# Five operand sums of a Strassen-form MoE layer moved to the tensor engine, and a Sinkhorn normalisation re-placed: one Trainium2 core

## The chip, the cores and the metric

The kernel runs on one core of one Trainium2 chip. The metric is the device time of one execution in microseconds (us): the kernel before takes 2233.35 us, the median of three runs (2232.98 to 2233.5). The times and views below come from the hardware profiler's record of one further execution, which took 2235.71 us, of which the span from the first to the last instruction is 2233.9 us.

## The reference, cut to what matters

```python
# banded attention with ALiBi slopes, 4 batches x 8 heads x 768 positions x 64
x = attention(q, k, v).transpose(0, 2, 1, 3).reshape(3072, 512)
logits = x @ w_gate                        # 3072 x 8
P = np.exp(logits - logits.max())
for _ in range(8):                         # Sinkhorn
    P /= P.sum(1, keepdims=True) + 1e-09   # rows
    P /= P.sum(0, keepdims=True) + 1e-09   # columns
    P *= N / E                             # 3072 / 8
out = 0
for e in range(8):                         # every expert, dense
    h  = np.maximum(x @ w1[e], 0.0)        # 512 -> 1024
    out += P[:, e:e+1] * (h @ w2[e])       # 1024 -> 512
```

All of it is float32. The column sums run over all 3072 rows, so no expert with a scale can be added up before the last token has been through attention and all eight iterations have ended.

## The kernel before, in words

**Precision.** An operand of a matmul is kept as a high part (rounded to the matmul's float32r format) and a low part (what is left), and a product is three matmuls: high x low, low x high, high x high (`products`, L601).

**Stages.** The 3072 rows are handled as 8 units of 384 rows (3 tiles of 128). `pipeline` (L750) first runs the attention unit by unit. Between its steps it fills in two kinds of work: the first half of expert 0 for the units already done (`filler`, L823: four first-layer tiles `h_ps`, L616, then three second-layer tiles `y_ps`, L683), and the operand sums for the Strassen form (`combine`, L584, its GpSimd branch, L596 to L599). Then comes the main part: the rest of expert 0 and experts 1 to 7, in 30 groups of 256 hidden columns, for three blocks of 1024 rows. The last block is done first, because its rows are still in SBUF (`passes`, L932).

**A group.** `layer1_strassen` (L630) makes the first layer of one group with seven products m1 to m7 of 6 matmuls each, into four PSUM banks a, b, c, d. The products take sums and differences of row tiles ("tile pairs"): m1, m6 and m7 take sums (`SUMS`, L761), m4 and m3 differences, which are written over the tiles they are made from (`DIFFERENCES`, L762). `second` (L946) then makes the second layer, 8 tiles of 6 matmuls, one group behind the first layer. From group 2 on (expert 1) each of its tiles is scaled by a column of `pm`, the Sinkhorn result (L962), and expert 0's part is scaled once (L961).

**The handover.** The last two tile pairs of the last block come from the last units of attention. Their three sums and two differences are made after attention, by `last_pairs` (L905), which calls `combine` with `hurry`: GpSimd adds the low parts (`xres`, L589), VectorE the high parts (`xsum`, L591) and the two together (L592), ScalarE rounds to the new high part (L593), VectorE subtracts to get the new low part (L594). In program order: the sums (L909), ten loads of sums made earlier (L910), the last unit's gate (L913), and the last unit's expert-0 filler (L916), with the differences between its two layers (L832), because they overwrite rows that the filler's first layer still reads.

**Sinkhorn.** `sinkhorn` (L716) is a generator. Each `next` issues one part: the maximum of the logits (three parts), then per iteration the row part (L735 to L738 on VectorE) and, in the next part, a matmul with ones for the column sums (`c_ps`, L741) and the column part (L743 to L747 on VectorE). Its sums `rsum` and `csum` are SBUF tiles. It takes 11 calls: four in the last filler (L918), the others in `second`, before every other tile (L955), from group 0's second layer on.

**What sets the order.** Each engine works through its own queue in order. The queues are written at compile time by a planner that simulates the program and takes, on each engine, what it thinks ready, earlier program order first. From group 3's first layer on, the tensor engine's matmuls stay in program order (`InOrder`, L79); the handover, Sinkhorn and groups 0 to 2 are in the planner's hands. PSUM in this part: four banks with tag "h" (`mps`, for `h_ps` and the banks a to d), three with tag "y" (`yps`), one with tag "s" (`sps`, for the gate and Sinkhorn).

Of the kernel before, what the change touches and what calls it, by code (L numbers as in the profile page):

```python
# [8 lines left out]
F32 = mybir.dt.float32  # L9
F32R = mybir.dt.float32r  # L10
I32 = mybir.dt.int32
AF = mybir.ActivationFunctionType
ALU = mybir.AluOpType
# [4 lines left out]
P = 128  # L18
# [483 lines left out]
class Moe:  # L502
# [4 lines left out]
    def __init__(self, tc, const, ident, w_gate, w1, w2, out):  # L507
        self.tc, self.nc = tc, tc.nc
        nc = self.nc
        self.ident, self.w1, self.w2, self.out = ident, w1, w2, out  # L510
        self.E, self.DM, self.DF = w1.shape
        self.KT = self.DM // P
        self.KH = self.KT // 2
        self.N = out.shape[0]
        self.NU = self.N // UNIT
        E = self.E
        self.g_f = const.tile([P, self.KT, E], F32, name="g_f")
        self.ghl = const.tile([P, self.KT, P], F32R, name="ghl")
        self.w_gate = w_gate
        self.ones = const.tile([P, P], F32, name="ones")  # L520
        nc.gpsimd.memset(self.ones, 1.0)
        TT = self.N // P
        self.lg = const.tile([P, TT, E], F32, name="lg")
        self.pm = const.tile([P, TT, E], F32, name="pm")
        self.small = const
        self.pe = nc.tensor

    def load_gate(self):
        nc, E, ghl = self.nc, self.E, self.ghl
        nc.sync.dma_start(out=self.g_f, in_=self.w_gate.rearrange("(c p) e -> p c e", p=P))  # L530
        nc.gpsimd.memset(ghl.bitcast(F32), 0.0)
        nc.gpsimd.tensor_copy(out=ghl[:, :, 0:E], in_=self.g_f)
        nc.gpsimd.tensor_tensor(out=ghl[:, :, E:2 * E], in0=self.g_f, in1=ghl[:, :, 0:E], op=ALU.subtract)

    def stage_pair(self, e, f, stage):
# [47 lines left out]

    def combine(self, dst, x, y, op, tmp, hurry):  # L584

        nc, n = self.nc, dst[0].shape[1]
        s = tmp.tile([P, 2, self.KH, P], F32, name="xsum")[:, 0:n]
        r = tmp.tile([P, 2, self.KH, P], F32, name="xres")[:, 0:n]
        nc.gpsimd.tensor_tensor(out=r, in0=x[1], in1=y[1], op=op)  # L589
        if hurry:  # L590
            nc.vector.tensor_tensor(out=s, in0=x[0], in1=y[0], op=op)  # L591
            nc.vector.tensor_tensor(out=s, in0=s, in1=r, op=ALU.add)  # L592
            nc.scalar.copy(out=dst[0], in_=s)  # L593
            nc.vector.tensor_tensor(out=dst[1], in0=s, in1=dst[0], op=ALU.subtract)  # L594
        else:
            nc.gpsimd.tensor_tensor(out=s, in0=x[0], in1=y[0], op=op)  # L596
            nc.gpsimd.tensor_tensor(out=dst[0], in0=s, in1=r, op=ALU.add)
            nc.gpsimd.tensor_tensor(out=s, in0=s, in1=r, op=ALU.add)
            nc.gpsimd.tensor_tensor(out=dst[1], in0=s, in1=dst[0], op=ALU.subtract)  # L599

# [28 lines left out]

    def layer1_strassen(self, x, w, hs, tmp, ps, tag, sums_first):  # L630

# [21 lines left out]
        if not sums_first:  # L653
            product("m1", "a", True, False)
        tt(out=h22, in0=a, in1=t3, op=ALU.add)
        if not sums_first:
            product("m6", "b", True, True)
        tt(out=b, in0=b, in1=h22, op=ALU.add)
        product("m5", "c", False, True)
        product("m4", "d", False, True)  # L660
        tt(out=t3, in0=d, in1=t3, op=ALU.add)
# [54 lines left out]
    def sinkhorn(self, ps, tag):  # L716
# [14 lines left out]
        nc.vector.tensor_scalar(out=gm, in0=ngm_ps, scalar1=-1.0, scalar2=None, op0=ALU.mult)  # L731
        nc.scalar.activation(out=pm, in_=lg, func=AF.Exp, bias=gm, scale=1.0)
        for _ in range(SINKHORN_ITERS):
            rsum = small.tile([P, TT], F32, name="rsum")
            nc.vector.tensor_reduce(out=rsum, in_=pm, op=ALU.add, axis=AX.X)  # L735
            nc.vector.tensor_scalar(out=rsum, in0=rsum, scalar1=EPS, scalar2=None, op0=ALU.add)
            nc.vector.reciprocal(out=rsum, in_=rsum)
            nc.vector.tensor_tensor(out=pm, in0=pm, in1=rsum.unsqueeze(2).broadcast_to([P, TT, E]), op=ALU.mult)  # L738
            yield
            c_ps = ps.tile([P, TT, E], F32, name="c_ps", tag=tag)  # L740
            self.pe.matmul(c_ps, lhsT=ones, rhs=pm, start=True, stop=True)  # L741
            csum = small.tile([P, E], F32, name="csum")
            nc.vector.tensor_reduce(out=csum, in_=c_ps.rearrange("p t e -> p e t"), op=ALU.add, axis=AX.X)  # L743
            nc.vector.tensor_scalar(out=csum, in0=csum, scalar1=EPS, scalar2=None, op0=ALU.add)
            nc.vector.reciprocal(out=csum, in_=csum)
            nc.vector.tensor_scalar(out=csum, in0=csum, scalar1=float(N) / E, scalar2=None, op0=ALU.mult)
            nc.vector.tensor_tensor(out=pm, in0=pm, in1=csum.unsqueeze(1).broadcast_to([P, TT, E]), op=ALU.mult)  # L747


def pipeline(tc, attention, ident, moe, acc, scratch):  # L750
# [12 lines left out]
    with ExitStack() as top:  # L763
# [23 lines left out]
        def block(m, c, n):  # L787

            k, i = BLOCKS[m]
            return tuple(ring[s][k][:, c + i:c + 2 * n:2] for s in range(2))  # L790
# [10 lines left out]
        def combo(m, x, y, op, p, n):  # L801
            c, b, q = 2 * p % RT, p // WT, slice(p % WT, p % WT + n)
            new = tuple(xout.tile([P, 2, KH, P], F32R, name=name)[:, 0:n] for name in ("oh", "ol"))
            moe.combine(new, block(x, c, n), block(y, c, n), op, xtmp, False)
            spills.extend((op_spill[b][m][s][:, q], new[s]) for s in range(2))
# [17 lines left out]
        def filler(u, ps1, tag1, ps2, tag2, dst=None):  # L823
# [7 lines left out]
            if dst is not None:  # L831
                last_pairs(DIFFERENCES, ALU.subtract, lambda m: block(m, LAST, 2))  # L832
            for t in range(UT):
# [70 lines left out]

        def last_pairs(ms, op, dst):  # L905
            for m, x, y in ms:
                moe.combine(dst(m), block(x, LAST, 2), block(y, LAST, 2), op, xtmp, True)

        last_pairs(SUMS, ALU.add, lambda m: tuple(a[:, 2:4] for a in ops[0][m]))  # L909
        for m in ("m1", "m6", "m7", "m4", "m3"):  # L910
            for s in range(2):
                dma(ops[0][m][s][:, 0:2], op_spill[NB - 1][m][s][:, 0:2])
        for _ in moe.gate(NU - 1, xs[NU - 1], sps, "s", sps, "s"):  # L913
            pass
        sinkhorn = moe.sinkhorn(sps, "s")
        for n, _ in enumerate(filler(NU - 1, mps, "h", yps, "y", acc[:, BT - UT:])):  # L916
            if n % 6 == 5:
                next(sinkhorn, None)  # L918
        fill.close()
# [26 lines left out]
        def second(g, b, hs):  # L946
            e = groups[g % NG][0]
            first_scaled = e != 0 and groups[g % NG - 1][0] == 0
            for i in range(2):
                for t in range(WT):  # L950
                    j = 2 * t + i
                    tt = b * BT + j
                    y_ps = moe.layer2(t, wts[g], hs[i], yps, "y")
                    if t % 2 == 0:
                        next(sinkhorn, None)  # L955
                    a = acc[:, j]
# [12 lines left out]
        for n, (g, b) in enumerate(steps):  # L969
# [3 lines left out]
            if p > 0 and g % NG == 0:  # L973
# [3 lines left out]
                prev = None  # L977
            hs = moe.layer1_strassen(ops[p % 2], wts[g], h_sets[n % 2], tmp, mps, "h", n == 0)
            if g + 1 < len(steps) and g + 1 not in wts:
# [79 lines left out]
```

## Time and profile before

| what | value |
|---|---|
| median of 3 runs | 2233.35 us |
| profiled execution, whole / span | 2235.71 / 2233.9 us |
| tensor engine busy | 2194.8 us (98%) |
| VectorE / GpSimd / ScalarE busy | 1358.9 / 1126.3 / 769.0 us |
| granted tensor clock, mean | 0.99 |
| end of attention and background filler on the tensor engine | about 344 us |
| first product of group 0 (m1) | 363.25 us |
| first and last Sinkhorn matmul | 371.85 and 448.13 us |
| first row block scaled by `pm` | 451.75 us |

A row of the timeline reads: start in us, duration in us, engine, source line, operation, output <- inputs, shape, count, and in brackets the idle time just before it with what ended it. PE is the tensor engine's matmul, PEld its weight load, DVE is VectorE, ACT ScalarE, POOL GpSimd, SP the queue that issues DMAs. A matmul's duration overlaps the next one's; what counts for throughput is the distance from start to start. L86 is a helper through which all in-order matmuls go. A tile's rows give minimum/median/maximum duration in ns. Rows of the windows view give busy time of each engine in a stretch, the number of instructions, and the granted tensor clock. The times lie in one execution, the median over three others.

### The profile page before, as it was taken

What the parts mean: (1) busy time and instruction counts of PE and PEld (TensorE: products, weight loads), DVE (VectorE), ACT (ScalarE), POOL (GpSimd) and SP (SyncE); (2) the same over time, 40 slices, a digit from 0 to 9 for tenths busy, and PEclk for the clock granted to TensorE, in tenths of its full rate; (3) what the DMA queues carried; (4) which work ended last, traced back from release to release, by engine and by line L of the source; (5) the groups of instructions that cost most, each with busy time, mean ns of one, the idle gap of its engine ahead of it and who ended that gap; (6) DMA issues with size and microseconds to landing.
All of it is one profiled execution on the core that took longest, in us unless ns stands there. A gap on an engine that the chain in (4) does not pass through costs nothing.

```text
span 2233.9 us, 29587 instructions
## 1 busy us (share of the span) xinstructions
PE 2194.8 (98%) x10887; PEld 1817.9 (81%) x10887; DVE 1358.9 (61%) x2382; ACT 769.0 (34%) x1562; POOL 1126.3 (50%) x1050
## 2 busy tenths in 40 slices
PE   8999998999999999999999999999999999999999
PEld 5888886778888888888888888888888888888887
DVE  5555556866566656655666666566556665666665
ACT  6676763223222322223222222222232232222221
POOL 5575575545454545445544545454555455544540
PEclk8999999999999999999999999999999999999999
DMA  6566554111111111162111111111521111111111
GB/s 157 160 168 180 150 161 162 39 48 48 57 48 57 48 57 48 57 221 89 49 49 55 51 54 48 57 48 57 167 88 47 57 48 57 48 51 54 50 46 49
DMA packets 224842, 177.68 MB, mean 80 GB/s; under 512 B 119728, under 2 KB 187824, under 8 KB 224688
## 3 DMA queue, kind: packets, MB, share of 16 engines
q1 hardware_dynamic: 224688, 175.70, 25.6%
q8 instruction: 87, 1.43, 0.3%
q14 instruction: 67, 0.55, 0.1%
HBM read 146.56 MB, written 29.10 MB: 79 GB/s over the span
## 4 chain that ended last, share of the span: by engine, by line
PE 93%; ACT 3%; DVE 3%; issue 1%; DMA 0%; SPq 0%; DVEq 0%; ACTq 0%
PE y_ps L86 45%; PE bank_a L86 11%; PE bank_d L86 10%; PE bank_c L86 10%; PE bank_b L86 5%; PE h_ps L86 2%; PE o_ps L86 2%; PE t_ps L89 2%; PE s_ps L86 1%; ACT p_sb L300 1%; PE tp L89 1%; DVE kl L249 0%; PE r_ps L89 0%; PE g_ps L86 0%; ACT kh L248 0%
## 5 line engine op out<-in xcount | busy, mean ns | idle before, releaser
L962 DVE SCALAR_TENSOR_TENSOR acc<-y_ps,pm,acc 128x512 f32<-128x512 f32 x672 | 502.7, 748 | 244.5 <-PE y_ps L86 243.3
L545 POOL TENSOR_TENSOR wl<-wsum,wh 128x1280 fp32r<-128x1280 f32 x90 | 266.1, 2957 | 556.2 <-ACT wh L544 556.2
L567 POOL TENSOR_TENSOR wsum<-w1f 128x256 f32<-128x256 f32 x450 | 318.0, 741 | 318.6 <-DMA w1f<-in_moe_w_dram 318.5
L86 PE MATMUL y_ps<-w2h,h_set 128*128 128x512 f32 x1408 | 434.7, 390 | 0.0
L86 PE MATMUL y_ps<-w2h,x 128*128 128x512 f32 x1408 | 433.5, 389 | 0.0
L544 ACT CAST w2h<-w2f 128x1024 fp32r<-128x1024 f32 x90 | 94.8, 1054 | 687.8 <-issue 612.2
L86 PEld LDWEIGHTS y_ps<-w2h,h_set 128*128 128x128 f32 x1408 | 265.2, 188 | 55.2
L86 PEld LDWEIGHTS y_ps<-w2h,x 128*128 128x128 f32 x1408 | 264.3, 188 | 54.9
L86 PE MATMUL y_ps<-w2l,h_set 128*128 128x512 f32 x704 | 274.9, 390 | 3.9 <-DVE acc L962 3.9
L86 PE MATMUL y_ps<-w2l,x 128*128 128x512 f32 x704 | 273.9, 389 | 0.0
L86 PE MATMUL bank_a<-m,wh 128*128 128x512 f32 x696 | 242.8, 389 | 1.0 <-DVE h_set L613 1.0
L545 POOL TENSOR_TENSOR w2l<-w2f,w2h 128x1024 fp32r<-128x1024 f32 x90 | 216.5, 2406 | 53.0 <-ACT w2h L544 53.0
L86 PE MATMUL bank_d<-x,wh 128*128 128x512 f32 x696 | 242.6, 389 | 0.0
L86 PE MATMUL bank_c<-x,wh 128*128 128x512 f32 x696 | 242.5, 389 | 0.0
L652 DVE TENSOR_TENSOR scratch<-scratch,bank_d 128x512 f32<-128x512 f32 x90 | 61.9, 688 | 175.1 <-PE bank_d L86 171.4
L86 PEld LDWEIGHTS y_ps<-w2l,h_set 128*128 128x128 f32 x704 | 132.7, 188 | 31.7 <-DVE acc L962 4.2
L86 PEld LDWEIGHTS y_ps<-w2l,x 128*128 128x128 f32 x704 | 132.1, 188 | 27.4
L86 PEld LDWEIGHTS bank_a<-m,wh 128*128 128x128 f32 x696 | 130.6, 188 | 29.0 <-DVE h_set L613 1.9
L86 PEld LDWEIGHTS bank_c<-x,wh 128*128 128x128 f32 x696 | 130.6, 188 | 27.1
L86 PEld LDWEIGHTS bank_d<-x,wh 128*128 128x128 f32 x696 | 130.6, 188 | 27.0
L86 PE MATMUL bank_a<-m,wl 128*128 128x512 f32 x348 | 135.4, 389 | 0.0
L86 PE MATMUL bank_d<-x,wl 128*128 128x512 f32 x348 | 135.4, 389 | 0.0
(230 smaller groups left out, 3568.4 us busy)
## 6 DMA issues: line engine op xcount, KB each, us to landing
w1f<-in_moe_w_dram SPq DMA_DIRECT2D x92, 512.0 KB, 3.4
w2f<-in_moe_w_dram SPq DMA_DIRECT2D x92, 512.0 KB, 3.6
x<-op_m SPq DMA_DIRECT2D x16, 512.0 KB, 7.9
m<-op_m SPq DMA_DIRECT2D x12, 512.0 KB, 8.1
out_dram<-acc SPq DMA_DIRECT2D x24, 256.0 KB, 4.0
ys<-y_sb SPq DMA_DIRECT2D x21, 256.0 KB, 2.2
acc<-ys SPq DMA_DIRECT2D x21, 256.0 KB, 4.1
op_m<-oh SPq DMA_DIRECT2D x30, 128.0 KB, 1.9
```

Of the source, the lines that this page charges most:

```text
L86: return self.tc.keep_in_program_order(self.engine.matmul(*args, **kw))
L89: return self.tc.keep_in_program_order(self.engine.transpose(*args, **kw))
L300: nc.scalar.activation(out=pv, in_=pv, func=AF.Exp, bias=mx[:, u:u + 1], scale=-1.0, accum_out=sm[:, i, j:j + 1])
L544: self.nc.scalar.copy(out=hi, in_=full)
L545: self.nc.gpsimd.tensor_tensor(out=lo, in0=full, in1=hi, op=ALU.subtract)
L567: nc.gpsimd.tensor_tensor(out=s[:, n], in0=x, in1=y, op=op)
L652: tt(out=t3, in0=t3, in1=d, op=ALU.subtract)
L962: nc.vector.scalar_tensor_tensor(out=a, in0=y_ps, scalar=moe.pm[:, tt, e:e + 1], in1=a, op0=ALU.mult, op1=ALU.add)
```

## The change

1. `combine` loses its `hurry` branch. A new `combine_fast` makes the last two pairs' sums and differences by four matmuls into one PSUM bank of tag "h": identity x high part of x, plus or minus identity x high part of y, and the same for the low parts. ScalarE rounds the bank to the new high part, VectorE subtracts for the new low part. GpSimd has no share in it. A constant `plus_minus` (identity and its negative) is made by two GpSimd instructions when the gate weights are loaded.
2. `last_pairs(SUMS, ...)` is called after the ten loads and the last unit's gate instead of before them.
3. In Sinkhorn, `rsum` and `csum` are columns of the same PSUM bank as `c_ps`, which is now allocated at the row part. The factor N/E is folded into the tensor_scalar ahead of the reciprocal (L744), so L746 goes.
4. `layer1_strassen` gets a `beat` that issues one part of Sinkhorn, called twice in each first layer; `second` issues a part before its tiles t == 2 only (two per group instead of four). The four calls in the last filler stay.

```diff
+        self.plus_minus = const.tile([P, 2, P], F32R, name="plus_minus")
...
+        nc.gpsimd.tensor_copy(out=self.plus_minus[:, 0], in_=self.ident)
+        nc.gpsimd.tensor_scalar(out=self.plus_minus[:, 1], in0=self.ident, scalar1=-1.0, scalar2=None, op0=ALU.mult)
...
+    def combine_fast(self, dst, x, y, minus, ps, tag):
+
+        nc = self.nc
+        s = ps.tile([P, 2, self.KH, P], F32, name="x_ps", tag=tag)
+        one, other = self.plus_minus[:, 0], self.plus_minus[:, int(minus)]
+        for m, (w, a) in enumerate(((one, x[0]), (other, y[0]), (one, x[1]), (other, y[1]))):
+            self.pe.matmul(s, lhsT=w, rhs=a, start=(m == 0), stop=(m == 3))
+        nc.scalar.copy(out=dst[0], in_=s)
+        nc.vector.tensor_tensor(out=dst[1], in0=s, in1=dst[0], op=ALU.subtract)
...
         if not sums_first:
             product("m1", "a", True, False)
+        beat()
         tt(out=h22, in0=a, in1=t3, op=ALU.add)
...
         product("m5", "c", False, True)
+        beat()
         product("m4", "d", False, True)
...
+        cols = TT * E
         for _ in range(SINKHORN_ITERS):
-            rsum = small.tile([P, TT], F32, name="rsum")
+            bank = ps.tile([P, cols + TT + E], F32, name="c_ps", tag=tag)
+            c_ps, rsum, csum = bank[:, 0:cols], bank[:, cols:cols + TT], bank[:, cols + TT:]
...
-            nc.vector.tensor_scalar(out=csum, in0=csum, scalar1=EPS, scalar2=None, op0=ALU.add)
+            nc.vector.tensor_scalar(out=csum, in0=csum, scalar1=EPS, scalar2=float(E) / N, op0=ALU.add, op1=ALU.mult)
             nc.vector.reciprocal(out=csum, in_=csum)
-            nc.vector.tensor_scalar(out=csum, in0=csum, scalar1=float(N) / E, scalar2=None, op0=ALU.mult)
...
-        last_pairs(SUMS, ALU.add, lambda m: tuple(a[:, 2:4] for a in ops[0][m]))
         for m in ("m1", "m6", "m7", "m4", "m3"):
             for s in range(2):
                 dma(ops[0][m][s][:, 0:2], op_spill[NB - 1][m][s][:, 0:2])
         for _ in moe.gate(NU - 1, xs[NU - 1], sps, "s", sps, "s"):
             pass
+        last_pairs(SUMS, False, lambda m: tuple(a[:, 2:4] for a in ops[0][m]))
         sinkhorn = moe.sinkhorn(sps, "s")
+
+        def beat():
+            next(sinkhorn, None)
...
-                    if t % 2 == 0:
-                        next(sinkhorn, None)
+                    if t == 2:
+                        beat()
```

More of the change, by code (lines that the diff above doesn't have):

```diff
@@ L582, in strassen_pair, with combine @@
         return wh, wl, w2h, w2l
-    def combine(self, dst, x, y, op, tmp, hurry):
+    def combine(self, dst, x, y, op, tmp):
         nc, n = self.nc, dst[0].shape[1]
@@ L589, in combine @@
         nc.gpsimd.tensor_tensor(out=r, in0=x[1], in1=y[1], op=op)
[L590 to L599, printed above, removed]
+        nc.gpsimd.tensor_tensor(out=s, in0=x[0], in1=y[0], op=op)
+        nc.gpsimd.tensor_tensor(out=dst[0], in0=s, in1=r, op=ALU.add)
+        nc.gpsimd.tensor_tensor(out=s, in0=s, in1=r, op=ALU.add)
+        nc.gpsimd.tensor_tensor(out=dst[1], in0=s, in1=dst[0], op=ALU.subtract)
+    def combine_fast(self, dst, x, y, minus, ps, tag):
[6 more added lines that the diff above has]
+        nc.vector.tensor_tensor(out=dst[1], in0=s, in1=dst[0], op=ALU.subtract)
     def products(self, out, hi, lo, xhi, xlo, n, first, last):
@@ L628, in layer1, with layer1_strassen @@
             yield 3 * UNIT
-    def layer1_strassen(self, x, w, hs, tmp, ps, tag, sums_first):
+    def layer1_strassen(self, x, w, hs, tmp, ps, tag, sums_first, beat):
         nc, KH = self.nc, self.KH
@@ L739, in sinkhorn @@
             yield
-            c_ps = ps.tile([P, TT, E], F32, name="c_ps", tag=tag)
             self.pe.matmul(c_ps, lhsT=ones, rhs=pm, start=True, stop=True)
-            csum = small.tile([P, E], F32, name="csum")
-            nc.vector.tensor_reduce(out=csum, in_=c_ps.rearrange("p t e -> p e t"), op=ALU.add, axis=AX.X)
-            nc.vector.tensor_scalar(out=csum, in0=csum, scalar1=EPS, scalar2=None, op0=ALU.add)
+            nc.vector.tensor_reduce(out=csum, in_=c_ps.rearrange("p (t e) -> p e t", e=E), op=ALU.add, axis=AX.X)
+            nc.vector.tensor_scalar(out=csum, in0=csum, scalar1=EPS, scalar2=float(E) / N, op0=ALU.add, op1=ALU.mult)
             nc.vector.reciprocal(out=csum, in_=csum)
-            nc.vector.tensor_scalar(out=csum, in0=csum, scalar1=float(N) / E, scalar2=None, op0=ALU.mult)
             nc.vector.tensor_tensor(out=pm, in0=pm, in1=csum.unsqueeze(1).broadcast_to([P, TT, E]), op=ALU.mult)
@@ L803, in combo @@
             new = tuple(xout.tile([P, 2, KH, P], F32R, name=name)[:, 0:n] for name in ("oh", "ol"))
-            moe.combine(new, block(x, c, n), block(y, c, n), op, xtmp, False)
+            moe.combine(new, block(x, c, n), block(y, c, n), op, xtmp)
             spills.extend((op_spill[b][m][s][:, q], new[s]) for s in range(2))
@@ L831, in filler @@
             if dst is not None:
-                last_pairs(DIFFERENCES, ALU.subtract, lambda m: block(m, LAST, 2))
+                last_pairs(DIFFERENCES, True, lambda m: block(m, LAST, 2))
             for t in range(UT):
@@ L903, in pipeline, with last_pairs @@
         ops[0].update({m: block(m, FIRST, WT) for m in BLOCKS})
-        def last_pairs(ms, op, dst):
+        def last_pairs(ms, minus, dst):
             for m, x, y in ms:
-                moe.combine(dst(m), block(x, LAST, 2), block(y, LAST, 2), op, xtmp, True)
-        last_pairs(SUMS, ALU.add, lambda m: tuple(a[:, 2:4] for a in ops[0][m]))
+                moe.combine_fast(dst(m), block(x, LAST, 2), block(y, LAST, 2), minus, mps, "h")
         for m in ("m1", "m6", "m7", "m4", "m3"):
@@ L953, in second @@
                     y_ps = moe.layer2(t, wts[g], hs[i], yps, "y")
-                    if t % 2 == 0:
-                        next(sinkhorn, None)
+                    if t == 2:
+                        beat()
                     a = acc[:, j]
@@ L977, in pipeline @@
                 prev = None
-            hs = moe.layer1_strassen(ops[p % 2], wts[g], h_sets[n % 2], tmp, mps, "h", n == 0)
+            hs = moe.layer1_strassen(ops[p % 2], wts[g], h_sets[n % 2], tmp, mps, "h", n == 0, beat)
             if g + 1 < len(steps) and g + 1 not in wts:
```

## The prediction

> **What bounds the kernel now.** I read the page first: is there an engine that is always busy?
>
> ```profile
> span 2233.9 us, 29587 instructions
> PE 2194.8 (98%) x10887; PEld 1817.9 (81%) x10887; DVE 1358.9 (61%) x2382; ACT 769.0 (34%) x1562; POOL 1126.3 (50%) x1050
> ```
>
> PE (the tensor engine) is. So work taken off DVE or POOL is worth nothing by itself; what counts is matmul time added and PE idle time removed. Next I cut the span into stretches around the places that the change touches, and asked what PE waits for in them.
>
> ```profile
> core 0: us, PE busy (x) PEld busy (x) DVE busy (x) ACT busy (x) POOL busy (x), PEclk, DMA share, GB/s
> 354.30:366.20 11.90, 11.83 (x52) 9.21 (x51) 6.31 (x11) 2.65 (x7) 7.57 (x8) 1.00 0.81 291
> 366.20:376.50 10.30, 1.03 (x3) 0.52 (x3) 9.05 (x13) 4.49 (x8) 6.78 (x5) 0.74 0.21 78
> 376.50:400.00 23.50, 23.38 (x91) 18.38 (x92) 16.31 (x34) 8.08 (x14) 11.71 (x14) 0.90 0.14 45
> 440.00:460.00 20.00, 12.43 (x47) 9.62 (x47) 13.86 (x25) 7.91 (x14) 7.90 (x8) 0.83 0.09 27
> 460.00:600.00 140.00, 140.00 (x619) 115.95 (x618) 86.39 (x124) 39.93 (x63) 68.18 (x58) 1.00 0.15 49
> ```
> ```profile
> PE c_ps L741 <- DVE pm L738: 9.4, 2, 5.7
> PE y_ps L86 <- DVE acc L962: 3.9, 1, 3.9
> PE bank_c L605 <- DVE x L594: 3.6, 1, 3.6
> PE y_ps L678 <- DVE acc L958: 0.9, 1, 0.9
> ```
>
> The first fence is the windows, the second all that PE waited for between 334 and 460 us. PE is full up to 366.2 and from 460 on. In between lie two holes, each followed by a stretch at less than the full granted clock, and one short wait. Between 366.2 and 376.5 PE does 1.03 us of work, in 440 to 460 it loses 7.6 us. Each wait ends on VectorE, on the lines that the change rewrites. The timeline of the first hole:
>
> ```profile
> 365.02 1.29 POOL L589 TENSOR_TENSOR xres<-x,x 128x512 f32<-128x512 f32 x1 [2.15 <-DMA m<-op_m]
> 365.74 0.39 PE L607 MATMUL bank_b<-m,wh 128*128 128x512 f32 x1
> 367.83 0.69 DVE L592 TENSOR_TENSOR xsum<-xsum,xres 128x512 f32<-128x512 f32 x1
> 368.69 2.89 POOL L545 TENSOR_TENSOR wl<-wsum,wh 128x1280 fp32r<-128x1280 f32 x1 [2.38 <-ACT wh L544]
> 368.77 3.03 DVE L738 TENSOR_TENSOR pm<-pm,rsum 128x192 f32<-128x192 f32 x1
> 371.85 1.01 PE L741 MATMUL c_ps<-pm,ones 128*128 128x192 f32 x2 [5.72 <-DVE pm L738]
> 373.29 2.10 DVE L744 TENSOR_SCALAR csum<-csum 128x8 f32<-128x8 f32 x1
> 375.74 0.68 DVE L594 TENSOR_TENSOR x<-xsum,x 128x512 fp32r<-128x512 f32 x1
> 376.48 0.79 PE L605 MATMUL bank_c<-x,wh 128*128 128x512 f32 x1 [3.62 <-DVE x L594]
> 381.61 0.49 PE L741 MATMUL c_ps<-pm,ones 128*128 128x192 f32 x2
> ```
>
> Group 0's m1 and m6 are done at 366. Its next product, m3, needs the last difference, whose low part (L594) is written only at 375.74, because it goes through POOL (L589), two DVE adds and a rounding, and its last step stands in DVE's queue behind Sinkhorn's. Sinkhorn's own steps are slow there: L738 starts 0.08 us after a POOL instruction and ends with it.
>
> ```profile
> L736 DVE TENSOR_SCALAR rsum<-rsum x8: 163/179/2030, 367.6 to 447.1; 128x24 f32<-128x24 f32 x8
> L738 DVE TENSOR_TENSOR pm<-pm,rsum x8: 343/358/3030, 368.8 to 447.6; 128x192 f32<-128x192 f32 x8
> L744 DVE TENSOR_SCALAR csum<-csum x8: 162/751/2341, 373.3 to 449.1; 128x8 f32<-128x8 f32 x8
> L735 DVE TENSOR_REDUCE rsum<-pm x8: 341/348/353, 366.8 to 446.7; 128x24 f32<-128x192 f32 x8
> L743 DVE TENSOR_REDUCE csum<-c_ps x8: 347/352/358, 372.9 to 448.7; 128x8 f32<-128x192 f32 x8
> L661 DVE TENSOR_TENSOR scratch<-bank_d,scratch x90: 681/691/692, 384.9 to 2205.4; 128x512 f32<-128x512 f32 x90
> L741 PE MATMUL c_ps<-pm,ones x16: 324/325/689, 371.9 to 448.4; 128*128 128x192 f32 x16
> ```
>
> What the reader is to see: an instruction that reads only SBUF operands (L736, L738, L744) is at times stretched to 2 or 3 us, one with a PSUM operand (L743, and L661, 90 times beside POOL's work) never. The column-sum matmuls run from 371.9 to about 448.1, eight iterations, 76.3 us for the seven distances, 10.9 each.
>
> ```profile
> 442.09 2.34 DVE L744 TENSOR_SCALAR csum<-csum 128x8 f32<-128x8 f32 x1
> 443.80 0.61 PE L86 MATMUL y_ps<-w2h,h_set 128*128 128x512 f32 x2
> 448.13 0.56 PE L741 MATMUL c_ps<-pm,ones 128*128 128x192 f32 x2 [3.71 <-DVE pm L738]
> 451.00 5.01 ACT L961 ACTIVATE acc<-acc,pm 128x512 f32<-128x512 f32 x8 [8.05 <-DVE pm L747]
> 452.56 0.79 PE L86 MATMUL y_ps<-w2l,h_set 128*128 128x512 f32 x1 [3.87 <-DVE acc L962]
> 456.55 0.40 PE L86 MATMUL y_ps<-w2l,h_set 128*128 128x512 f32 x1
> 461.48 1.36 PE bank_c L86 x6
> ```
>
> The second hole: group 2's second layer has filled its three "y" banks at 444.3 and can't go on until `pm` is final, 451. The last row (from the chain of waits) gives the price of a matmul with 512 columns at full clock: 1.36 / 6 = 0.227 us.
>
> **The change, part by part.** *The holes, as sums.* First: the matmul after 365.74 would have started at 365.97; bank_c starts at 376.48, so 10.5 us, less about 0.3 for the c_ps pair that stays (my estimate from its 0.325 us rows) = 10.2. Then 12 matmuls take 381.61 - 376.48 = 5.13 us for 12 x 0.227 = 2.72: 2.4 us of low clock. Together 12.6. Second: the next start would be 443.80 + 2 x 0.227 = 444.25; it is 452.56, so 8.3 - 0.3 = 8.0, and nine matmuls to 456.55 take 3.99 for 2.04: 1.95. Together 9.95. The short wait on L958: 0.9. All three: 23.4 us, the most that the change can save.
>
> *Added on PE.* Five combinations of four matmuls with 512 columns: 20 x 0.227 = 4.5 us. They fall between 344 and 363, where PE has no gap (row 354.30:366.20), so all of it is paid. The weights are a constant and come with each matmul as everywhere else. Were PE to take them inside a remaining hole, they would cost 0; above 4.5 only at low clock, 9.1.
>
> *The differences.* In program order they stand behind the filler's first layer and ahead of its second layer.
>
> ```profile
> 354.48 0.39 PE L691 MATMUL y_ps<-w2l,hh 128*128 128x512 f32 x1
> 363.02 0.39 PE L693 MATMUL y_ps<-w2h,hh 128*128 128x512 f32 x1
> ```
>
> After their 8 matmuls PE has this second layer (8.8 us) and m1 and m6 (12 x 0.227 = 2.7 us) to do before m3: 11.5 us of cover for one rounding and one subtraction per difference, about 0.69 us each by L592 and L594. They will be ready some 8 us early. Without the cover (a DVE queue held up by 8 us) the first hole comes back from its start. What was the next late thing behind them? m1's sums were there at 363, and the weights of group 1 are being split in the hole itself (L545 at 368.69), with the whole of group 0's first layer, 42 x 0.227 = 9.5 us, still ahead of their use. POOL loses five L589 (1.3 us and more each) and is earlier. The ten loads go to SP's queue ahead of the sums instead of behind them, which can only bring them forward. The sums take three "h" banks ahead of the filler's four `h_ps`; each comes free after a rounding and a subtraction, 1.4 us, while the other banks still take 0.9 to 2 us of matmuls each. I take 0 to 2 us.
>
> *The constant.* Two POOL instructions of 128x128 beside the gate weights' split; the nearest row has eight times the elements, so they cost well under its 1.04 us each, early, where POOL waits for weights:
>
> ```profile
> 24.82 1.04 POOL L554 CAST w1h<-w1f 128x1024 fp32r<-128x1024 f32 x1 [1.94 <-DMA w1f<-in_moe_w_dram]
> ```
>
> It idles 1.94 us there: 0.
>
> *Sinkhorn in PSUM.* With a PSUM operand in each of the stretched lines, the stretches go: by the medians 3.03 - 0.36, 2.03 - 0.18 and 2.34 - 0.18 us for the worst three alone. One instruction of nine per iteration (L746) goes too. [...]
>
> *Sinkhorn's parts.* After the four calls in the filler, two calls in each first layer and two in group 0's second layer end it in group 2's first layer; before, the eleventh call came in group 1's second layer. What matters is whether `pm` is final before PE has filled the three "y" banks of group 2. That point moves from 444.25 to 444.25 - 12.6 - 0.9 + 4.5 = 435.3. The first c_ps moves from 371.85 to about 365 (the end of the filler, 363.25 + 4.5, less the four last of its 28 pieces). From the last c_ps to PE's restart are 452.56 - 448.13 = 4.4 us. So seven distances have 435.3 - 4.4 - 365 = 65.9 us, 9.4 each. Before they took 10.9, but with the stretches in them (L744's median is 751 ns against a minimum of 162) and with a distance that waited for a call in group 0's second layer. The ends are 10.9, the distance now, and 1.24, the medians of L735, L736, L738 and L743 alone, with no queue between them. The nearest row is the first distance, 371.85 to 381.61: 9.8, less L744's stretch (2.10 - 0.18) 7.8. I take 8 to 9, since DVE gets busier after it. That is close to the limit, and the weakest step here.
>
> *What I hold back.* c_ps stands in PE's queue where the planner thought `pm` ready; everything behind it on PE waits with it. Two of eight waited before. With Sinkhorn's steps now also between DVE's bank work of groups 0 and 1 (DVE 16.31 of 23.5 us busy), I put 2 us for such waits and for banks that come free later, with bounds of 0 and 9.4 (the waits on L738 now).
>
> *Sum.* 2235.7 (the profiled execution, 1.8 outside the span) - 23.4 + 4.5 + 2 = 2218.8. The median of the runs lies 2.4 below that execution, so 2216.4; I write 2216.5. Its own range: 2212 (nothing held back, small gains) to 2221.
>
> **The rivals.** *A. `pm` is late again.* The distances stay near 10.9: the last c_ps at 365 + 76.3 = 441, PE restarts at 446 instead of 435, and the second hole stands as it was. Gain 12.6 + 0.9 - 4.5 = 9 us less 1: 2225. For it: the first distance is 7.8 even with its stretch taken out, and the planner, not the chip, sets PE's order. Against: Sinkhorn's steps now precede the competing DVE work in program order.
>
> *B. The first hole changes its owner.* The differences are early, but the first c_ps, placed behind m6, still waits for `pm` (5.7 of its 10 us now). Say half the hole and its low clock stay, 6.3 us: 2223. Against: the exponential's inputs waited on DVE behind the sums that leave it.
>
> *C. Slower.* Place: PE's queue, at the eight c_ps. The planner puts them close behind the steps that feed them, in first layers where PE has nothing else it may do, and DVE is late each time. It decides from a mean wait of (23.4 - 4.5) / 8 = 2.4 us; at the shorter of the waits seen, 3.71, eight are 29.7: 2233.35 - 18.9 + 29.7 = 2244. Against: six of eight had no wait with a slower DVE.
>
> *D. No effect:* the planner reorders so that m3 waits for something as late as now, and the 4.5 us are paid against one small gain: 2231 to 2236.
>
> **How the numbers follow.** Forecast 0.62, A 0.18, B 0.10, C 0.04, D 0.06. The range of 8 in 10 runs from 2211.5 to A's upper side, 2227. A measurement of this kernel tells about 0.2% (4.5 us) from no change. Faster by more: forecast, A, B and a little of D, 0.91; within: most of D and the low end of C, 0.05; slower: 0.04.
>
> **What would show it.** Right: PE busy in each stretch between 345 and 450 with no idle over 1 us; 20 new matmuls of 0.39 us; no row of DVE with a PSUM operand over 0.75 us; last c_ps before 431 and the first L962 with no PE wait before it; granted clock 1.00 throughout. Wrong: an idle stretch of PE of over 3 us anywhere from 345 to 450, waits at c_ps, stretched rows at L736, L738 or L744, or a loss after 460, where nothing is touched.

## The result, and the profile after

The changed kernel takes 2261.28 us (median of 4 runs, 2258.6 to 2262.01); the kernel before, beside it, 2233.18 us (2232.98 to 2233.5). The ratio is 1.0121, 95% interval [1.0109, 1.0133]: 28 us slower, where 17 us faster was forecast. The profiled execution took 2261.53 us, its span 2259.7.

From the page of the kernel after: the span, the busy times, and the shares of the chain that ended last.

```profile
span 2259.7 us, 29605 instructions
PE 2236.5 (99%) x10907; PEld 1818.5 (80%) x10907; DVE 1333.9 (59%) x2364; ACT 768.4 (34%) x1562; POOL 1119.8 (50%) x1047
PE 96%; ACT 2%; DVE 1%; issue 0%; DMA 0%; SPq 0%; ACTq 0%; DVEq 0%
```

PE does 20 matmuls more than before, as it should, but is busy 41.7 us longer, and the chain that sets the end is 96% PE: almost nothing in it is a wait. The windows of the kernel after, PE alone (stretch, length, busy time and matmuls, granted clock, DMA share, GB/s), and all that PE waited for from 334 to 460 us:

```profile
360.00:380.00 20.00, 19.75 (x86) 1.00 0.43 145
440.00:460.00 20.00, 20.00 (x87) 1.00 0.09 32
460.00:600.00 140.00, 140.00 (x605) 1.00 0.16 52
600.00:1000.00 400.00, 400.00 (x1726) 1.00 0.23 76
```
```profile
PE bank_c L612 <- DVE h_set L620: 0.2, 1, 0.2
```

Both holes are gone, the clock is 1.00 in them, and 0.2 us of waiting is left of the 17.8 that the four waits of before add up to. But in 140 us of uninterrupted work after them PE starts 605 matmuls, where it started 619. The same window of the kernel before, further on:

```profile
600.00:1000.00 400.00, 400.00 (x1766) 1.00 0.22 73
```

1726 for 1766: 2.3% fewer, at the same full clock, with no idle time in either. (The next rows do not depend on such a count.) One group of instructions gives an exact yardstick: the second layer's matmuls out of the second set of first-layer results, which the profile calls x. Its first start is the first such tile after the handover, its last nearly the end of the kernel, and the same work lies between them in every kernel here. The tile view of y_ps, before and after (minimum/median/maximum in ns, first and last start in us); the row above it is the last of attention and background filler:

```profile
L86 PE MATMUL y_ps<-w2h,x x1408: 388/389/389, 471.1 to 2228.1; 128*128 128x512 f32 x176
L86 PE MATMUL y_ps<-w2h,hh x84: 388/393/401, 87.1 to 343.9; 128*128 128x512 f32 x84
```
```profile
L86 PE MATMUL y_ps<-w2h,x x1408: 390/393/404, 452.6 to 2253.9; 128*128 128x512 f32 x176
L86 PE MATMUL y_ps<-w2h,hh x84: 387/393/403, 86.4 to 343.0; 128*128 128x512 f32 x84
```

This splits the time into two numbers, used for every run below. **The handover**, from 343.9 to 471.1, took 127.2 us before and takes 452.6 - 343.0 = 109.6: 17.6 us gained. **The main part**, from the first to the last start of the x row, took 2228.1 - 471.1 = 1757.0 us and takes 2253.9 - 452.6 = 1801.3: 44.3 us lost. With 0.9 us from the earlier end of attention that is -0.9 - 17.6 + 44.3 = 25.8, the whole difference of the two spans (2259.7 - 2233.9). So the change did to the handover what was foretold, and something slowed the main part by 2.5%, though no operation of it was edited. The row itself shows it: 389 at minimum, median and maximum alike before, but for 1 ns; 390/393/404 after.

Where it begins is seen in the timeline of the kernel after, at group 0's first products (the first matmul of each bank's six):

```profile
368.60 0.39 PE L612 MATMUL bank_b<-m,wh 128*128 128x512 f32 x1
369.96 0.40 PE L612 MATMUL bank_c<-x,wh 128*128 128x512 f32 x1
371.35 0.40 PE L612 MATMUL bank_d<-x,wh 128*128 128x512 f32 x1
```

Six matmuls into bank b take 1.36 us, 0.227 each as before; the next six, into bank c, 1.39, with weights out of the same tile, no wait and the same clock. What differs is the operand. `m` here is one of the sums; it lies in the right side of SBUF, like the weights `wh`. `x` lies in the left side. The tile allocator fills the left side from one end and the right side from the other. The new constant `plus_minus` takes 1024 bytes per partition on the left, and `rsum` and `csum`, which are gone, took 96 + 32. So every later tile on the left (the operand tiles, the first layer's results, the weight staging) has moved by 1024 - 128 = 896 bytes, and nothing on the right. In the compiled programs the first `x` tile starts at byte 48256 of a partition before and at 49152 after, the lower of the two `wh` tiles at 159616 in both (the other lies 88 times 256 bytes above it). This became the theory: **the distance between the addresses of a matmul's two operands sets its pace.** Its rivals: PE's pace is left over from how it came out of the handover (with or without a hole); the new calls of Sinkhorn's parts, or some other part of the new order, slow it; or only the absolute place of the left tiles counts.

### The profile page after: what moved, and what is told of

The parts are those of the page before. It is cut to its first block, busy times and chain, and to the rows that moved or that the text cites. A ratio compares the mean times of both kernels' runs of the same rounds, so it can differ in the third digit from the quotient of the medians.

```text
span 2259.7 us, 29605 instructions
## 1 busy us (share of the span) xinstructions
PE 2236.5 (99%) x10907; PEld 1818.5 (80%) x10907; DVE 1333.9 (59%) x2364; ACT 768.4 (34%) x1562; POOL 1119.8 (50%) x1047
## 4 chain that ended last, share of the span: by engine, by line
PE 96%; ACT 2%; DVE 1%; issue 0%; DMA 0%; SPq 0%; ACTq 0%; DVEq 0%
PE y_ps L86 46%; PE bank_a L86 11%; PE bank_d L86 11%; PE bank_c L86 11%; PE bank_b L86 5%; PE h_ps L86 2%; PE o_ps L86 2%; PE t_ps L89 2%; PE s_ps L86 2%; PE tp L89 1%; ACT p_sb L300 1%; PE g_ps L86 0%; PE r_ps L89 0%; DVE kl L249 0%; PE y_ps L688 0%; PE y_ps L689 0%
## 5 line engine op out<-in xcount | busy, mean ns | idle before, releaser
L86 PE MATMUL y_ps<-w2h,x 128*128 128x512 f32 x1408 | 441.5, 395 | 0.0
L86 PE MATMUL y_ps<-w2h,h_set 128*128 128x512 f32 x1408 | 441.5, 395 | 0.0
L86 PE MATMUL bank_c<-x,wl 128*128 128x512 f32 x348 | 136.9, 393 | 0.0
```

The lines of the kernel that those rows point to most:

```text
L86: return self.tc.keep_in_program_order(self.engine.matmul(*args, **kw))
```

## The experiments

In all of them the full result is computed. The padded tiles have columns that nothing reads.

**1. The kernel after, its left side moved on to a full 1024 bytes.** 128 bytes are added behind `ones`; every engine's instructions are the same as after, in the same order.

```diff
-        self.ones = const.tile([P, P], F32, name="ones")
+        self.ones = const.tile([P, P + 32], F32, name="ones")[:, 0:P]
```

> The kernel after, with the constant `ones` 128 bytes a partition longer and nothing else. Every tile that is allocated after it on the left side of SBUF (the ring x, the sums of the second block, h_set, w1f) then lies 1024 bytes above its place in the kernel before, instead of 896; the tiles on the right side (wh, wl, w2h, w2l) lie where they were in both. All engines' instructions are the same and in the same order. Theory addresses: a matmul with 512 columns takes 227 ns from start to start or about 232 by how its two SBUF operands lie to each other, and the shift of 896 bytes spoilt it; 1024 restores it: 2216 us (2211 to 2222), spacing 227 ns. Theory stall: the spacing depends on whether PE has come out of a hole at low clock (the kernel before had two, the kernel after none) and not on addresses: 2261 us, spacing 232 ns.

Measured: 2214.5 us (2213.76 to 2215.8; before beside it 2233.69), ratio 0.9917 [0.9901, 0.9934]. The tile view and the timeline:

```profile
L86 PE MATMUL y_ps<-w2h,x x1408: 388/389/389, 449.3 to 2206.2; 128*128 128x512 f32 x176
L86 PE MATMUL y_ps<-w2h,hh x84: 388/394/401, 84.2 to 340.9; 128*128 128x512 f32 x84
```
```profile
366.59 0.39 PE L612 MATMUL bank_b<-m,wh 128*128 128x512 f32 x1
367.96 0.39 PE L612 MATMUL bank_c<-x,wh 128*128 128x512 f32 x1
369.32 0.39 PE L612 MATMUL bank_d<-x,wh 128*128 128x512 f32 x1
```

The main part takes 2206.2 - 449.3 = 1756.9 us, as before, and bank c's six now take 1.36. 128 unused bytes are worth 46.8 us (2261.28 - 2214.5), and this kernel is faster than both the kernel before and the kernel after. The handover takes 108.4 us, 1.2 less than in the kernel after, since the slow pace began inside it.

**2. The kernel before, with nothing but the shift.** 896 bytes behind `ones`; order unchanged.

```diff
-        self.ones = const.tile([P, P], F32, name="ones")
+        self.ones = const.tile([P, P + 224], F32, name="ones")[:, 0:P]
```

> The kernel before, with the constant `ones` 896 bytes a partition longer and nothing else: the left side of SBUF lies as in the kernel after, with the order of all instructions as in the kernel before, the two holes included. Theory addresses: about 8,200 matmuls each some 5 ns slower after 376 us, 2270 to 2280 us, spacing about 232 ns from 460 us on. Theory stall: no change, 2233 us, spacing 227 ns.

Measured: 2279.59 us (2277.2 to 2280.4), ratio 1.0205 [1.0188, 1.0222]. Windows of PE and the tile view:

```profile
360.00:380.00 20.00, 10.79 (x40) 0.74 0.32 106
440.00:460.00 20.00, 12.27 (x41) 0.74 0.09 27
600.00:1000.00 400.00, 400.00 (x1726) 1.00 0.19 63
```
```profile
L86 PE MATMUL y_ps<-w2h,x x1408: 390/393/405, 470.0 to 2271.4; 128*128 128x512 f32 x176
```

The two holes are there as in the kernel before, and the main part is slow as in the kernel after: 1801.4 us, 1726 matmuls from 600 to 1000. The first experiment has no hole and is fast. So how PE comes out of the handover has no say in it; that rival falls, and no edit of the change but its bytes is needed for the loss.

**3. The kernel after, the right side moved instead.** 128 bytes in the first tile of the right side shift the weights by -128; the left side stays where it is in the kernel after.

```diff
-    edge = ctx.enter_context(tc.tile_pool(name="edge", bufs=1, side="right")).tile([P, 24], F32, name="edge")
+    edge = ctx.enter_context(tc.tile_pool(name="edge", bufs=1, side="right")).tile([P, 24 + 32], F32, name="edge")
```

> The kernel after, with the first tile of the right side (`edge`) 128 bytes longer: the weights wh, wl, w2h, w2l and the first block's sums move down by 128 bytes, the left side stays as in the kernel after. Left and right then lie to each other as in the kernel before, modulo 1024 bytes. Theory addresses, relative form (what counts is the distance between the two operands modulo 1024 bytes or a divisor): 2216 us, spacing 227 ns. Theory addresses, absolute form (what counts is that x begins on a multiple of 1024 bytes): 2261 us, 232 ns. Theory stall: 2261 us.

Measured: 2215.34 us (2213.73 to 2216.15), ratio 0.9917 [0.99, 0.9934].

```profile
L86 PE MATMUL y_ps<-w2h,x x1408: 388/389/390, 451.3 to 2208.3; 128*128 128x512 f32 x176
```

1757.0 us: fast, with the left tiles at the very addresses that were slow. What counts is the distance, not the place.

**4. The kernel after with the old calls of Sinkhorn's parts.**

```diff
-        beat()
...
-                    if t == 2:
+                    if t % 2 == 0:
```

> The kernel after, with Sinkhorn's parts called where the kernel before calls them (no beat in the first layers, four in each second layer); addresses as in the kernel after. The hole ahead of the first scaled rows should come back in part. Theory addresses: spacing stays 232 ns, and the time is 2261 us plus a hole of 3 to 10 us: 2264 to 2271. [...]

Measured: 2262.66 us (2260.9 to 2262.84), ratio 1.0128 [1.0112, 1.0145]. PE's waits from 334 to 460, and the tile view:

```profile
PE y_ps L86 <- DVE acc L973: 1.5, 1, 1.5
PE bank_c L612 <- DVE h_set L620: 0.2, 1, 0.2
```
```profile
L86 PE MATMUL y_ps<-w2h,x x1408: 390/393/404, 453.5 to 2254.9; 128*128 128x512 f32 x176
L86 PE MATMUL y_ps<-w2h,hh x84: 387/393/403, 85.9 to 342.5; 128*128 128x512 f32 x84
```

The main part stays at 1801.4, so the calls aren't the cause. The handover takes 111.0 for 109.6: the new calls are worth 1.4 us, the wait of 1.5 us for `pm` that comes back, where a hole of 3 to 10 was expected.

**5. Other shifts of the left side in the kernel after,** by 16, 64 and 96 columns behind `ones` (64, 256 and 384 bytes); one run each, on another chip, where the kernel before took 2229.31 us.

```diff
-        self.ones = const.tile([P, P], F32, name="ones")
+        self.ones = const.tile([P, P + 16], F32, name="ones")[:, 0:P]
```

> The kernel after with `ones` 64 bytes longer, nothing else: the ring x lies 192 bytes beyond a multiple of 1024 from the weights wh on the right side (kernel before and the fast runs: 256; kernel after: 128). If only multiples of 256 are fast: some 232 ns from start to start in the main part and about 2260 us. If the distance need only be off 128, or if what counts is finer (32 or 64 bytes): 227 ns, 2215 us. Something between would say that the loss is graded.

> The kernel after with `ones` 256 bytes longer: distance of x to wh 384 bytes modulo 1024. If what counts is the distance modulo 256 (384 is 128 beyond): slow as the kernel after, 232 ns, 2261 us. If it counts modulo 1024, or 128 alone is bad: 227 ns, 2215 us.

> The kernel after with `ones` 384 bytes longer: distance of x to wh 512 bytes modulo 1024. If what counts is the distance modulo 256: fast, 227 ns, 2215 us. If only the kernel before's own distance (256 modulo 1024) and 0 are fast: slow, 2261 us.

Measured: 2249.64, 2262.07 and 2215.12 us. The tile view of each in that order:

```profile
L86 PE MATMUL y_ps<-w2h,x x1408: 388/394/398, 452.4 to 2241.0; 128*128 128x512 f32 x176
```
```profile
L86 PE MATMUL y_ps<-w2h,x x1408: 390/393/404, 452.7 to 2254.1; 128*128 128x512 f32 x176
```
```profile
L86 PE MATMUL y_ps<-w2h,x x1408: 388/389/389, 450.5 to 2207.5; 128*128 128x512 f32 x176
```

1788.6, 1801.4 and 1757.0 us. Among these shifts not the size but the remainder modulo 256 decides: 384 bytes are as good as 128, 256 as bad as none, and the distance 192 costs the main part 31.6 us where 128 costs 44.4.

**6. The weights moved away from the sums too.** Experiment 1, plus a gap of 128 bytes on the right between the sums and the weights (and one GpSimd instruction that fills it). Now both `x` and `m` are 128 bytes off.

```diff
-        self.ones = const.tile([P, P], F32, name="ones")
+        self.ones = const.tile([P, P + 32], F32, name="ones")[:, 0:P]
...
+        gap = top.enter_context(tc.tile_pool(name="gap", bufs=1, side="right", reuse_waits="tile"))
+        nc.gpsimd.memset(gap.tile([P, 32], F32, name="gap"), 0.0)
```

> The kernel e1 (left side 1024 bytes above the kernel before, fast) with 128 bytes put between the right side's sums and the weights, so that wh, wl, w2h, w2l alone move by 128 bytes; the sums m on the right side and everything on the left stay where they were in the fast run. Distances modulo 256 then are 128 for x to wh, for h_set and x to w2, and also for the first block's sums to wh. If what counts is how the two operands of a matmul lie to each other: slow, 232 ns, about 2260 us, and slow in the products m1, m6, m7 of the first block too, which in the kernel after are the fast ones. If the left side's own place counts, or its place against the sums or acc: fast, 2215 us. One memset of 128x32 on GpSimd comes with it, under 1 us and off the path.

Measured: 2266.58 us, one run. The timeline and the tile view:

```profile
367.13 0.40 PE L612 MATMUL bank_b<-m,wh 128*128 128x512 f32 x1
368.52 0.40 PE L612 MATMUL bank_c<-x,wh 128*128 128x512 f32 x1
369.92 0.39 PE L612 MATMUL bank_d<-x,wh 128*128 128x512 f32 x1
```
```profile
L86 PE MATMUL y_ps<-w2h,x x1408: 387/398/398, 451.3 to 2258.9; 128*128 128x512 f32 x176
```

Bank b, fast in the kernel after with the same operands, now takes 1.39 us for its six like the others, and the main part, 1807.6 us, is the slowest of all. The runs that moved tiles, in one table (bytes per partition, the distance from the compiled addresses):

| kernel | left tiles | weights | distance x to wh, modulo 256 | main part, us |
|---|---|---|---|---|
| before | 0 | 0 | 0 | 1757.0 |
| after | +896 | 0 | 128 | 1801.3 |
| experiment 1 | +1024 | 0 | 0 | 1756.9 |
| experiment 2 | +896 | 0 | 128 | 1801.4 |
| experiment 3 | +896 | -128 | 0 | 1757.0 |
| 5, 64 bytes | +960 | 0 | 192 | 1788.6 |
| 5, 256 bytes | +1152 | 0 | 128 | 1801.4 |
| 5, 384 bytes | +1280 | 0 | 0 | 1757.0 |
| experiment 6 | +1024 | -128 | 128 (and `m` to wh) | 1807.6 |

**7. The parts of the change, each alone on the kernel before,** with the distance kept at 0: what did each give in the handover? *The combinations on PE alone* (parts 1 and 2 of the change; its shift is 1024 by itself):

```diff
+        self.plus_minus = const.tile([P, 2, P], F32R, name="plus_minus")
...
-                moe.combine(dst(m), block(x, LAST, 2), block(y, LAST, 2), op, xtmp, True)
+                moe.combine_fast(dst(m), block(x, LAST, 2), block(y, LAST, 2), minus, mps, "h")
```

> The kernel before with the tensor-engine sums and differences alone (its constant, its place after the gate); Sinkhorn's sums stay in SBUF and its parts where they were. The constant alone shifts the left side by 1024 bytes, which leaves the distances modulo 1024 as before: fast spacing. By the prediction's sum: the first hole goes (12.6 us) but c_ps may still wait for a stretched L738 there, 20 matmuls come (4.5 us), the second hole stays: 2233.4 - 12.6 + 4.5 = 2225, with 2220 to 2232 as bounds. A rival: the first hole was Sinkhorn's as much as the differences', and half of it stays: 2231.

*Sinkhorn's sums in PSUM alone* (part 3; 128 bytes behind `ones` make up for the two tiles that go):

```diff
-            rsum = small.tile([P, TT], F32, name="rsum")
+            bank = ps.tile([P, cols + TT + E], F32, name="c_ps", tag=tag)
+            c_ps, rsum, csum = bank[:, 0:cols], bank[:, cols:cols + TT], bank[:, cols + TT:]
```

> The kernel before with Sinkhorn's sums in PSUM alone (and one instruction fewer per iteration); `ones` 128 bytes longer so that all other tiles lie where they were. The stretched rows of L736, L738 and L744 go, some 13 us over eight iterations. By the prediction: the second hole (9.95 us) shrinks by its 2.2 us stretch and what the earlier ones delayed, 3 to 8 us, the first by the stretches in it, 3 to 5 us: 2221 to 2228. A rival: the planner's order sets the places of c_ps, so PE waits as long: 2231 to 2234.

*The new calls alone* (part 4):

```diff
+        beat()
...
-                    if t % 2 == 0:
+                    if t == 2:
```

> The kernel before with Sinkhorn's parts called in the first layers alone; sums in SBUF, combine as before, all tiles where they were. If the second hole was set by the place of the calls: it goes, 2233.4 - 10 = 2223. If it was set by the stretched instructions: c_ps still waits for them, earlier: 2230 to 2236, or slower if several c_ps wait.

*Sums in PSUM and new calls together* (the two edits above):

```diff
+            c_ps, rsum, csum = bank[:, 0:cols], bank[:, cols:cols + TT], bank[:, cols + TT:]
...
-                    if t % 2 == 0:
+                    if t == 2:
```

> The kernel before with both Sinkhorn edits (sums in PSUM, parts in the first layers) and combine as before; tiles where they were. The second hole goes (9.95 us) and with it the short wait (0.9); in the first hole the differences still come through GpSimd and VectorE, so the part of it that ends on L594 stays, 5 to 12 us of 12.6: 2233.4 - 10.9 - 0 to 7 = 2215 to 2223, middle 2219. With p1 it says whether the two gains add up to e1's 19 us.

Measured, against 2233.27 us for the kernel before, with the handover as above (first start of the x row less last of the hh row):

| kernel | us | ratio | handover, us |
|---|---|---|---|
| before | 2233.27 | 1 | 127.2 |
| combinations alone | 2222.34 | 0.995 [0.9934, 0.9967] | 116.0 |
| sums in PSUM alone | 2220.51 | 0.9943 [0.9926, 0.9959] | 113.4 |
| new calls alone | 2233.45 | 0.9999 [0.999, 1.0009] | 126.9 |
| sums and calls | 2220.65 | 0.9941 [0.9924, 0.9957] | 112.5 |
| all, distance 0 (experiment 1) | 2214.5 | 0.9917 [0.9901, 0.9934] | 108.4 |

What PE waited for most from 334 to 460 in the combinations alone, in the sums alone and in the calls alone:

```profile
PE y_ps L86 <- DVE acc L969: 3.8, 1, 3.8
PE bank_c L612 <- DVE h_set L620: 1.3, 1, 1.3
```
```profile
PE c_ps L742 <- DVE pm L740: 2.5, 1, 2.5
PE bank_c L605 <- DVE x L594: 2.4, 1, 2.4
PE y_ps L86 <- DVE acc L961: 1.5, 1, 1.5
```
```profile
PE c_ps L744 <- DVE pm L741: 8.9, 2, 5.4
PE y_ps L86 <- DVE acc L969: 3.7, 1, 3.7
PE bank_c L605 <- DVE x L594: 3.6, 1, 3.6
```

The combinations remove the first hole but for 1.3 us and leave the second's wait (3.8). The sums shorten all three waits, those of the first hole too. The calls alone do nothing: the waits are where they were. The sums alone did slightly more than the 2221 to 2228 us expected of them. And the gains do not add up: the combinations give 11.2 us of handover, sums and calls 14.7, all together 18.8, because both shorten both holes. Of 9.3 us of waiting in the first the combinations leave 1.3 and the sums 4.9, of 7.6 in the second 3.8 and 1.5. What the sums change is seen on VectorE, in the rows of the combinations alone (sums in SBUF) and of the sums alone (in PSUM):

```profile
L745 DVE TENSOR_TENSOR pm<-pm,rsum x8: 340/434/2848, 360.3 to 428.7; 128x192 f32<-128x192 f32 x8
L751 DVE TENSOR_SCALAR csum<-csum x8: 164/1064/1949, 366.2 to 433.8; 128x8 f32<-128x8 f32 x8
```
```profile
L740 DVE TENSOR_TENSOR pm<-pm,c_ps x8: 344/352/356, 366.3 to 429.6; 128x192 f32<-128x192 f32 x8
L744 DVE TENSOR_SCALAR c_ps<-c_ps x8: 164/170/175, 367.8 to 435.8; 128x8 f32<-128x8 f32 x8
```

The same two steps go up to 2.85 and 1.95 us in the one, and never over 0.356 in the other. GpSimd is at work beside them in both: of the 24 rows of the three lines that were stretched (L736, L738 and L744 of the kernel before, eight iterations), 14 lie for over half their time beside a GpSimd instruction of 0.3 us or more in the combinations alone. Ten of these 14 take over 0.6 us, and no other row does. In the sums alone 15 lie so, and none is stretched. The kernels before and after show the same: before, 10 of the 24 lie so, seven of these take over 0.6 us and no other row does; after, 13 lie so, and the longest of the 24 takes 0.357 us.

## Why the prediction was wrong, point by point

**The step that failed** is "*Sum.*": its terms end before 460, and the main part stands in it at nothing, because no operation there is edited. The price of a matmul, 1.36 / 6 = 0.227 us, was taken as fixed, when it held only for the distances of the kernel before. And "a loss after 460, where nothing is touched" was listed as a sign of being wrong, but with no term and no rival behind it: all of A to D lie between 345 and 450. What the runs showed in its place is 44.3 us: the left side of SBUF moved by 896 bytes, which isn't a multiple of 256, and the untouched matmuls slowed. "*The constant.*" was the place to see it: it counted two GpSimd instructions, found cover for them, wrote 0, and left out the 1024 bytes. But these alone cost the main part nothing. The combinations alone bring the same constant and move the left side by 1024, and their main part takes 2214.5 - 457.5 = 1757.0 us:

```profile
L86 PE MATMUL y_ps<-w2h,x x1408: 388/389/390, 457.5 to 2214.5; 128*128 128x512 f32 x176
```

It is the 128 bytes that `rsum` and `csum` gave up which make 896 of the 1024 (the sums in PSUM without bytes that make up for them were not run). The main part in the trace of before runs at distance 0 and shows 389 ns throughout, so it gave no such price. That the addresses move could be read from the diff.

**The rest of the sum held.** It said 23.4 saved and 4.5 paid, 18.9 in all, less 2 held back. With the distance at 0 the handover falls from 127.2 to 108.4, by 18.8, and the median is 2214.5, where 2216.5 was forecast. The 2 us held back for waits at `c_ps` were not needed. (The trace of experiment 1 is 21.8 us shorter than that of before; the other 3.0 are the earlier end of attention, 340.9 for 343.9, which no edit touches.) Step by step, in the tile views of x_ps and c_ps of the kernel after:

```profile
L604 PE MATMUL x_ps<-x,plus_minus x20: 388/392/394, 344.6 to 357.9; 128*128 128x512 f32 x20
L752 PE MATMUL c_ps<-pm,ones x16: 323/325/327, 366.7 to 431.7; 128*128 128x192 f32 x16
L748 DVE TENSOR_SCALAR c_ps<-c_ps x8: 180/191/192, 361.1 to 426.1; 128x24 f32<-128x24 f32 x8
L750 DVE TENSOR_TENSOR pm<-pm,c_ps x8: 343/354/357, 361.7 to 426.7; 128x192 f32<-128x192 f32 x8
L754 DVE TENSOR_SCALAR c_ps<-c_ps x8: 165/174/175, 367.6 to 432.7; 128x8 f32<-128x8 f32 x8
```

- *The combinations:* 20 matmuls of 0.39 us between 344.6 and 357.9, from 0.228 to 0.230 us from start to start, paid as foretold, and the differences early enough for bank c at 369.96, right behind bank b.
- *Sinkhorn in PSUM:* no stretched row is left; the three lines that went up to 2.03, 3.03 and 2.34 us are at most 0.192, 0.357 and 0.175. What a step pays for an operand in PSUM stands in the sum at nothing; the trace of before had 352 ns for 192 values from PSUM (L743) and 348 for as many from SBUF (L735). By the medians of after no step is over 14 ns longer than in the trace of before (L749, 316 ns for the 302 of L737), and the seven steps besides L744 and L746 come to 2149 ns an iteration for 2100, where L746's 172 are gone. Experiment 7 agrees with the reason: the stretches go where the sums alone are put in PSUM (one instruction an iteration goes with that edit), and stay in the combinations alone.
- *The distances of `c_ps`:* (431.7 - 366.7) / 7 = 9.3 us, where 8 to 9 was taken and 9.4 was the limit. The first one starts at 366.7, where 365 was taken, and the last at 431.7, not "before 431". The slowing is 0.8 us of that and no more: counted from the last start of the hh row (343.0) the last `c_ps` is at 88.7 us, and in experiment 1, without the slowing (340.9), at 87.9, where the mark stands at 431 - 343.9 = 87.1. So nothing was left to spare: in the kernel after, the fourth tile of group 2's second layer starts at 435.54, some 0.2 us after the matmuls ahead of it would have let it. That no second hole came of it is in part luck. The row of experiment 1:

```profile
L752 PE MATMUL c_ps<-pm,ones x16: 324/324/325, 364.7 to 428.8; 128*128 128x192 f32 x16
```

- *What brings them closer* was put down to the place of the calls as well as to the stretches. The calls alone leave the distances at 10.9 us ((445.8 - 369.4) / 7). The sums alone bring them to 9.7 ((434.5 - 366.7) / 7), but so do the combinations alone, with the stretches still in them: 9.6 ((432.3 - 365.3) / 7). Each of these two edits shortens them, then, and the stretches are not all that made them long. That the distances also held PE's own holes, which both edits shorten, would fit; it was not measured by itself. With the sums the calls still leave 1.5 us of waiting, as the sums have by themselves; only with the combinations as well do they take that away (experiment 4). The row of PE's waits in sums and calls together:

```profile
PE y_ps L86 <- DVE acc L968: 1.5, 1, 1.5
```

- *The owner of the first hole* was too simply drawn. It was given to the late differences alone, with Sinkhorn's wait as a possible heir (rival B). Both were in it: the sums in PSUM by themselves already shorten it (2.4 us are left of 3.6 at bank c and 2.5 of 5.7 at c_ps), and the combinations by themselves take away the wait at c_ps too, with Sinkhorn's sums still in SBUF.

None of the rivals came true: A and B, since no wait over 0.2 us is left; C, since no c_ps waits; D, since the holes are gone. The slower result came from outside them.

## What to carry to other kernels

A change that adds or drops an SBUF tile, even one of 128 bytes, moves all tiles allocated behind it, and can change the pace of the matmuls that have one operand among the moved tiles and one among the others: here a pad of 128 bytes took the main part from 1801.3 us to 1756.9. The cause was two small tiles dropped, beside a constant that alone would have done no harm. Compare the tile view's minimum, median and maximum of an untouched matmul group, and its first and last start, before anything else: if an untouched group got slower at the same clock with no waits, try a pad of 128 bytes before judging the change. Here the pad turns 1.2% slower into 0.8% faster.

## What the runs showed of the hardware that was not expected

Two matmul streams with the same instructions, the same clock (1.00) and no idle time (400.00 of 400 us busy from 600 to 1000 us in the kernels before and after) differ in pace by the distance of their stationary and moving operands within a partition: at 256 or 512 bytes modulo 1024 the main part takes 1756.9 to 1757.0 us, at 128 or 384 it takes 1801.3 to 1801.4 (1807.6 where the sums are off as well), and at 192 it takes 1788.6. All of that fits a period of 256 bytes. Another stream shows the remainder 64: the matmuls of the combinations have both operands on the left, `x` and `plus_minus` (from byte 44480). The first twelve take 2.74 us from their start to that of the next matmul in the kernel after (344.60 to 347.34), where the remainder (`x` less `plus_minus`, modulo 256) is 64; 2.78 in experiment 5 with 64 bytes (344.54 to 347.32), where it is 128; and 2.80 in experiment 1 (342.56 to 345.36), where it is 192. So the operands need not lie on different sides, and the slowest of the remainders tried isn't the same in both streams (192 in the main part, and 128 here, are one run each). Steps under 64 were not tried. Moving either operand restores the pace (1756.9 us in experiment 1, 1757.0 in experiment 3). Why the distance matters is not shown: the trace has no view of SBUF's reads, and no run measured a read by itself.
